# Token groups of 512 and 640 with more staging and scratch buffers, a plain third product and a schedule made anew, in a fused attention and multiplicative feed-forward kernel

## The chip, the cores and the metric

The kernel runs on one core of a Trainium2 chip. The metric is the device time of one execution in microseconds (us), the median of several runs. The profile adds a span, from the first to the last instruction, which is some 1.9 us shorter than the device time. The engines are named as in the profile: PE (TensorE, matmuls), PEld (its weight loads), DVE (VectorE), ACT (ScalarE), POOL (GpSimd), SP (SyncE, which here issues the loads and most of the stores).

## The reference, cut to what matters

```python
q_s = exp(q - max(q));  q_s = q_s / sum(q_s, over head_dim)      # q, k, v: 8 x 8 x 576 x 64
k_s = exp(k - max(k));  k_s = k_s / sum(k_s, over seq)
kv   = einsum('bhsd,bhse->bhde', k_s, v)
attn = einsum('bhsd,bhde->bhse', q_s, kv)
x = attn.transpose(0, 2, 1, 3).reshape(4608, 512)
h = ((x @ w1) * (x @ w2)) @ w3                                   # 512 x 1024, 512 x 1024, 1024 x 1024
out = h @ w_out                                                  # 1024 x 512
```

There are eight batches of 576 tokens, 4608 tokens in all.

## The kernel before

The program first multiplies w3 by w_out once (`W3O`), so that each token needs only `x@w1`, `x@w2`, the product of the two, and one third product with `W3O`. The tokens are worked off in groups. The first group takes its first two products in the plain form. The later groups take them in a form with seven half-width multiplications in place of eight, which costs additional adds on DVE, scratch (`uu`, `cc`) and input combinations (`tt`). In group 4 the third product of eight tiles has such a form as well (`S2S`).

```python
GROUPS = [(0, 576), (576, 576), (1152, 1024), (2176, 640), (2816, 1024), (3840, 768)]
S2S = {4: 4}
HM = max(n for _, n in GROUPS) // 2
tiles("st", 9, [P, 2 * RK * D], F32)      # staging of every load
tiles("tt", 6, [P, 2, HM])
tiles("ab", 18, [P, 1024])
tiles("uu", 5, [P, HM], F32)
tiles("cc", 6, [P, HM])
tiles("ps", 8, [P, 512], F32, psum)

# ... the plain form of the first two products (first group)
for ct in (2 * n, 2 * n + 1):
    nc.tensor.matmul(ps.tile[:, 0:m], lhsT=w[qt][:, ct, fo:fo + P],
                     rhs=x[:, ct, lo:lo + m], start=(ct == 0), stop=(ct == 3))

# ... the third product, plain
for ft in (2 * n, 2 * n + 1):
    nc.tensor.matmul(po.tile[:, :w], lhsT=ab_buf[(g, ft)].tile[:, tb * P:(tb + 1) * P],
                     rhs=W3O[:, ft, m * w:(m + 1) * w], start=(ft == 0), stop=(ft == N_FT - 1))

# ... warm-up matmuls: they compute nothing that is used
def fill(ps, n):
    for _ in range(n):
        nc.tensor.matmul(ps[:, 0:512], lhsT=blank[:, 0:P], rhs=blank, start=True, stop=True)
```

Nothing is scheduled at run time. The tasks (a load, a cast, a pair of matmuls, an eviction) are numbered. A fixed list `ORDER` gives their sequence, `SLOTS` the buffer of each, and `ENGS` the engine of each task that several engines could do.

```python
def run(self, order, slots, engs):
    for b, s in zip(self.bufs, slots):
        b.tile = self.pools[b.pool][s]
    for n in order:
        if isinstance(n, tuple):
            self.fill(self.pools[n[0]][n[1]], n[2])      # warm-up matmuls
        elif self.tasks[n].alts:
            self.tasks[n].emit(engs[n])
        else:
            self.tasks[n].emit()
```

Each engine runs its own instructions in that sequence, so an early instruction that waits holds back all later ones of the same engine.

The softmax here doesn't subtract the row's maximum and nothing guards it: scores larger than these inputs give would overflow.

## Time and profile before

| | before |
|---|---|
| device time, median of the runs beside the changed kernel | 231.76 us (231.07 to 232.23, 4 runs) |
| span of the profiled run, mean granted clock | 230.0 us, 1.0 |
| PE work: useful, warm-up matmuls | 204.0 us, 5.8 us |
| nothing issued on PE | 20.2 us |
| first dense run of first-layer matmuls starts | 33.87 us |

PE work in the table is the order of the PE instructions with columns/2.4 + 3 ns for each, as the prediction derives it. The rest of the span is called unissued: PE had nothing to do, or ran below full pace. Below, the first 34 us are called the head, the handing over from one group of tokens to the next a handover, and what lies between the head and the last third-product matmuls the middle. Here is the memory traffic line of the page of before: GB/s moved in each of 40 equal slices of the span, 5.75 us each.

```profile
GB/s 222 390 404 391 392 388 268 379 330 13 353 371 333 158 242 278 372 50 337 180 211 171 278 278 171 128 111 297 274 204 165 75 0 48 24 68 92 116 131 165
```

After the first slice, the loads run at about 390 GB/s without a break for five slices, to 34.5 us.

### The profile page before, as it was taken

To read this page: it belongs to the slowest core of one execution; us is meant where nothing else is said; L and a number is where in the kernel's file an instruction comes from. 1 tells how busy PE (TensorE), PEld (TensorE's weight loads), DVE (VectorE), ACT (ScalarE), POOL (GpSimd) and SP (SyncE) were. 2 spreads that over 40 slices of the span, in tenths; PEclk is the share of its full clock that TensorE was granted. 3 is DMA by queue.
4 is the path that set the end of the run, shared out by engine and by line. 5 is a ranking of instruction groups with operands and counts; after the bars stand their busy time and mean duration, and the time that the engine had idled before them with its cause. 6 is when DMAs were issued, how large, how long until landed. Compare 5 with 4: busy or idle time off the path is not lost.

```text
span 230.0 us, 5284 instructions
## 1 busy us (share of the span) xinstructions
PE 219.9 (96%) x1971; PEld 124.6 (54%) x1971; DVE 182.8 (79%) x392; ACT 142.0 (62%) x289; POOL 102.2 (44%) x84
## 2 busy tenths in 40 slices
PE   7699999999999999999999999999999899999992
PEld 3354548866676564444445656543444367766640
DVE  0332865789999998999967989999999999889820
ACT  2236875768768998777527658766799474354021
POOL 4313745584064990197940268800299920310000
PEclk9999999999999999999999999999999999999999
DMA  6999997981998679919786976669885502124556
GB/s 222 390 404 391 392 388 268 379 330 13 353 371 333 158 242 278 372 50 337 180 211 171 278 278 171 128 111 297 274 204 165 75 0 48 24 68 92 116 131 165
DMA packets 32888, 50.92 MB, mean 221 GB/s; under 512 B 11744, under 2 KB 12000, under 8 KB 32864
## 3 DMA queue, kind: packets, MB, share of 16 engines
q1 hardware_dynamic: 31504, 48.57, 66.5%
q10 hardware_dynamic: 1360, 2.03, 3.8%
q8 instruction: 15, 0.25, 0.5%
q14 instruction: 9, 0.07, 0.1%
HBM read 38.80 MB, written 9.44 MB: 210 GB/s over the span
## 4 chain that ended last, share of the span: by engine, by line
PE 72%; DVE 10%; DMA 8%; ACT 3%; issue 2%; POOL 2%; SPq 2%; DVEq 0%; ACTq 0%
PE ps L648 31%; PE ps L739 17%; PE ps L591 7%; PE ps L377 6%; PE ps L836 5%; DMA st<-in_moe_w_dram 3%; DMA out_dram<-osb 2%; DMA qsT<-eq 2%; DVE cc L672 2%; PE ps L511 2%; PE ps L556 2%; DVE tt L626 2%; DVE ds L459 1%; POOL eq L469 1%; PE ps L485 1%
## 5 line engine op out<-in xcount | busy, mean ns | idle before, releaser
L672 DVE TENSOR_TENSOR cc<-ps,uu 128x512 f16<-128x512 f32 (+3 forms) x120 | 65.2, 570 | 2.8 <-PE ps L648 0.7
L344 ACT COPY uu<-ps 128x512 f32<-128x512 f32 (+3 forms) x107 | 50.4, 501 | 25.9 <-PE ps L648 14.9
L699 POOL TENSOR_TENSOR ab<-cc,cc 128x512 f16<-128x512 f16 (+3 forms) x25 | 23.1, 927 | 70.2 <-DVE cc L672 59.4
L739 PE MATMUL ps<-W3O,ab 128*128 128x512 f16 (+1 forms) x224 | 53.4, 372 | 0.0
L648 PE MATMUL ps<-tt,wc 128*128 128x512 f16 (+3 forms) x240 | 52.1, 334 | 0.3
L648 PEld LDWEIGHTS <-wc 128*128 128x128 f16 x320 | 31.0, 98 | 25.6 <-DVE tt L626 1.4
L648 PE MATMUL ps<-xt,w 128*128 128x512 f16 (+3 forms) x160 | 36.6, 334 | 0.5 <-ACT osb L725 0.5
L648 PEld LDWEIGHTS <-w 128*128 128x128 f16 x240 | 22.6, 98 | 18.1 <-issue 1.8
L739 PEld LDWEIGHTS <-ab 128*128 128x128 f16 x224 | 21.4, 98 | 20.1 <-issue 0.6
L469 POOL TENSOR_TENSOR eq<-eq,ds 128x1152 f16<-128x1152 f16 x13 | 27.9, 2152 | 6.6 <-DVE ds L466 3.3
L725 ACT ACTIVATE osb<-ps 128x512 f32<-128x512 f32 (+1 forms) x24 | 13.3, 566 | 22.5 <-PE ps L739 19.9
L459 DVE TENSOR_REDUCE ds<-eq 128x9 f32<-128x576 f16 x32 | 23.4, 740 | 4.0 <-ACT eq L455 4.0
L672 DVE TENSOR_TENSOR ab<-ps,cc 128x512 f16<-128x512 f32 (+3 forms) x40 | 22.4, 567 | 1.8 <-PE ps L648 0.6
L455 ACT ACTIVATE eq<-st 128x576 f16<-128x576 f32 x32 | 21.5, 686 | 1.1 <-DMA st<-in_q_dram 1.0
L434 ACT ACTIVATE ek<-st 128x576 f16<-128x576 f32 x32 | 21.0, 688 | 1.6 <-DMA st<-in_k_dram 1.3
L344 ACT CAST xt<-ps 128x320 f16<-128x320 f32 (+7 forms) x46 | 15.4, 400 | 9.1 <-PE ps L556 8.9
L648 PE MATMUL ps<-xt,wc 128*128 128x512 f16 (+3 forms) x80 | 20.2, 334 | 0.0
L648 PE MATMUL ps<-tt,w 128*128 128x512 f16 (+3 forms) x80 | 19.7, 334 | 0.0
L591 PE MATMUL ps<-xt,w 128*128 128x320 f16 (+1 forms) x128 | 16.2, 286 | 0.0
L377 PE MATMUL ps<-ab,ab 128*128 128x512 f16 x64 | 14.8, 379 | 0.4 <-ACT ab L344 0.3
L591 PEld LDWEIGHTS <-w 128*128 128x128 f16 x128 | 12.3, 98 | 3.6 <-issue 0.2
L344 POOL CAST v<-st 128x1152 f16<-128x1152 f32 x10 | 12.5, 1261 | 0.8 <-PE ps L511 0.8
(76 smaller groups left out, 251.6 us busy)
## 6 DMA issues: line engine op xcount, KB each, us to landing
st<-in_q_dram SPq DMA_DIRECT2D x16, 576.0 KB, 5.3
st<-in_v_dram SPq DMA_DIRECT2D x16, 576.0 KB, 8.0
st<-in_k_dram SPq DMA_DIRECT2D x16, 576.0 KB, 7.2
st<-in_moe_w_dram SPq DMA_DIRECT2D x16, 512.0 KB, 8.9
out_dram<-osb SPq DMA_DIRECT2D x56, 128.0 KB, 4.1
st<-in_moe_w_out_dram SPq DMA_DIRECT2D x4, 512.0 KB, 7.5
out_dram<-osb ACTq DMA_DIRECT2D x14, 128.0 KB, 2.4
out_dram<-osb ACTq DMA_DIRECT2D x3, 64.0 KB, 2.5
```

The source lines that it names most:

```text
L344: {"DVE": nc.vector.tensor_copy, "POOL": nc.gpsimd.tensor_copy, "ACT": nc.scalar.copy}[eng](out=o, in_=i)
L377: nc.tensor.matmul(pp.tile, lhsT=wT.tile[:, gt * P:(gt + 1) * P], rhs=wo[i][1].tile[:, (gt % 2) * C:(gt % 2 + 1) * C], start=(gt == 0), st ...
L434: nc.scalar.activation(out=ek.tile[:, :, j, :], func=AF.Exp, in_=vk(bk.tile)[:, j].rearrange("p (r d) -> p r d", r=RK))
L455: nc.scalar.activation(out=eq.tile[:, :, j, :], func=AF.Exp, in_=vq(bq.tile)[:, j].rearrange("p (r d) -> p r d", r=RK))
L459: nc.vector.tensor_reduce(out=ds.tile[:, 0, j], axis=AX.X, op=ALU.add, in_=eq.tile[:, :, j, :])
L469: {"POOL": nc.gpsimd, "DVE": nc.vector}[e].tensor_tensor(out=eq.tile, in0=eq.tile, op=ALU.mult, in1=ds.tile[:, 1].rearrange("p j r -> p r ...
L591: nc.tensor.matmul(ps.tile[:, 0:m], lhsT=w[qt][:, ct, fo:fo + P], rhs=x[:, ct, lo:lo + m], start=(ct == 0), stop=(ct == 3))
L648: nc.tensor.matmul(ps.tile[:, 0:h], lhsT=lhs(c), rhs=rhs(c), start=first and c == 0, stop=c == 1, skip_group_check=not first)
L672: return lambda: nc.vector.tensor_tensor(out=dst(), in0=ps.tile[:, 0:h], in1=other.tile[:, 0:h], op=op)
L699: {"POOL": nc.gpsimd, "DVE": nc.vector}[e].tensor_tensor(out=ab.tile[:, 0:h], in0=c11.tile[:, 0:h], in1=c21.tile[:, 0:h], op=ALU.mult)
L725: nc.scalar.activation(out=o(), in_=i(), func=AF.Copy, scale=ISC)
L739: nc.tensor.matmul(po.tile[:, :w], lhsT=ab_buf[(g, ft)].tile[:, tb * P:(tb + 1) * P], rhs=W3O[:, ft, m * w:(m + 1) * w], start=(ft == 0), ...
```

## The change

The intent: groups of about one batch each, so that less work is bunched at a handover from one group to the next; smaller half widths, whose saved memory pays for more staging and scratch buffers; and a third product in plain form, which spares DVE the combinations.

```diff
-    GROUPS = [(0, 576), (576, 576), (1152, 1024), (2176, 640), (2816, 1024), (3840, 768)]
+    GROUPS = [(0, 512), (512, 640), (1152, 512), (1664, 640), (2304, 512), (2816, 640), (3456, 512), (3968, 640)]
-    S2S = {4: 4}
+    S2S = {}
-    tiles("st", 9, [P, 2 * RK * D], F32)
+    tiles("st", 10, [P, 2 * RK * D], F32)
-    tiles("tt", 6, [P, 2, HM])
+    tiles("tt", 8, [P, 2, HM])
-    tiles("uu", 5, [P, HM], F32)
-    tiles("cc", 6, [P, HM])
+    tiles("uu", 7, [P, HM], F32)
+    tiles("cc", 7, [P, 512])
 # ... cut: helper code for cases that this configuration doesn't use
 # ... cut: ORDER, SLOTS and ENGS are new throughout: another sequence of loads, casts and
 #          matmuls from the first instruction on, and 19 warm-up matmuls in place of 27
```

The last comment matters. The lists were made anew for the new groups, and with them the first 35 us changed, although the loads and casts of the weights, which fill most of that time, do not depend on the groups.

## The prediction

> **What bounds the kernel now.** I read the page's busy line first, then the windows by stage, then the groups by form, then the chain of work that ended last.
>
> The busy line of the page says that PE is the fullest engine and DVE the second:
>
> ```profile
> PE 219.9 (96%) x1971; PEld 124.6 (54%) x1971; DVE 182.8 (79%) x392; ACT 142.0 (62%) x289; POOL 102.2 (44%) x84
> ```
>
> 96% overstates PE, because matmul spans overlap. So I first worked out the pace of PE. Below are one stretch of ten microseconds that holds only 512-column matmuls (columns: stretch and length, then busy and count for PE, PEld, DVE, ACT, POOL, then clock, DMA share, GB/s), and lines of the chain (start, length, what):
>
> ```profile
> 100.00:110.00 10.00, 10.00 (x47) 4.44 (x46) 9.40 (x16) 7.21 (x14) 8.47 (x8) 1.00 0.67 219
> ```
>
> ```profile
> 2.13 7.04 DMA st<-in_moe_w_dram
> ...
> 33.87 14.48 PE ps L591 x118
> ...
> 217.48 8.01 PE ps L739 x42
> 225.53 0.60 ACT osb L725
> ```
>
> 47 matmuls in 10 us is 0.213 us each (0.216 allowing for one at the edge), and 118 of 320 and 256 columns in equal parts take 14.48 us, 0.1227 each. Both fit columns/2.4 ns plus 3 ns. With that pace, the whole instruction order of before is 209.8 us of PE work: weight product 17.5, attention 14.2 (64x64 pieces run four at a time, 72 in 0.78 us), first two products 111.5, third product 60.8, warm-up matmuls 5.8. Laying this work along the timeline leaves 20.2 us with nothing issued: 5.2 in the first 10 us, 2.6 more up to 33.87, 7.8 spread from there to the last matmul (183.7 us of work in the 191.5 us to 225.4), and 4.6 from there to the end. The middle is therefore already tight, and a gain can only come from the unissued time.
>
> Now the stages of before, cut roughly where the groups follow each other:
>
> ```profile
> 34.00:59.00 25.00, 24.81 (x263) 17.28 (x262) 19.43 (x45) 17.11 (x33) 14.11 (x7) 1.00 0.71 251
> 59.00:89.00 30.00, 29.91 (x378) 19.44 (x377) 27.59 (x71) 25.66 (x60) 16.89 (x14) 1.00 0.83 283
> 89.00:125.00 36.00, 35.79 (x313) 16.44 (x310) 31.42 (x56) 23.45 (x43) 18.41 (x12) 1.00 0.74 229
> 125.00:158.50 33.50, 33.04 (x286) 18.41 (x287) 31.23 (x74) 22.71 (x55) 14.84 (x11) 1.00 0.77 203
> 158.50:184.00 25.50, 24.80 (x193) 10.79 (x191) 24.81 (x44) 19.70 (x39) 18.47 (x15) 1.00 0.74 197
> 184.00:217.50 33.50, 33.47 (x243) 23.37 (x240) 30.47 (x72) 14.12 (x37) 4.19 (x5) 1.00 0.24 56
> 0.00:34.00 34.00, 30.15 (x267) 15.05 (x268) 15.10 (x32) 17.19 (x26) 14.34 (x20) 1.00 0.97 364
> ```
>
> The reader should see DVE at 24.81 of 25.5 us in one stage and 31.2 of 33.5 in another, but 19.4 of 25 in the first. DMA is at 0.97 only up to 34 us. So there are three regimes: loads until about 33 us, then PE and DVE together, then a tail of third-product matmuls and stores.
>
> The groups by form give the DVE price against width:
>
> ```profile
> L672 DVE TENSOR_TENSOR cc<-ps,uu 128x512 f16<-128x512 f32 x48 | 31.3, 681 | 0.6 <-ACT uu L344 0.2
> L672 DVE TENSOR_TENSOR cc<-ps,uu 128x384 f16<-128x384 f32 x24 | 12.9, 552 | 1.2 <-PE ps L648 0.5 <-POOL ab L699 0.2
> L672 DVE TENSOR_TENSOR cc<-ps,uu 128x320 f16<-128x320 f32 x24 | 11.0, 483 | 0.2
> L672 DVE TENSOR_TENSOR cc<-ps,uu 128x288 f16<-128x288 f32 x24 | 10.0, 451 | 0.8 <-PE ps L648 0.3 <-ACT uu L344 0.2
> ```
>
> That is 1.03 ns a column plus 155 ns. The durations of all DVE rows sum to 204 us against 182.8 busy, so neighbours overlap by some 54 ns, and an extra instruction really costs about 100 ns.
>
> **What the Trainium skill says.** "TensorE: Matmul & The Clock Gate", section "Back-to-back issue gap", gives an isolated gap of N/2.4 + 2.5 ns and a sustained 131 ns at N=512. The first agrees with this trace, the second does not: 213 to 217 ns here. "VectorE: DVE Perf Modes", the section on the TRN2 errata, says a fixed cost comes with each instruction, (N+151)/0.96 ns for an fp32 add, and advises tiles of 512 or more; the rows above agree (681 ns against its 691). "Perfetto Trace Analysis", section "Optimization Strategy", recommends interleaving regimes with different limits, and says that repeated bubbles can mean too few buffers. Both describe the intent of the change.
>
> **The change, part by part.** Counts are from the built instruction orders of the two kernels.
>
> Third product. The seven-multiplication form in group 4 goes (112 matmuls of 256 columns, 28,672 columns), and 32,768 columns in plain form come in. On PE, third product 60.8 to 62.3 us: +1.5. In return DVE loses 12 combining evictions at 418 ns (5.0 us), 8 half sums (3.3) and 3 scalings (1.3), and POOL loses 12 combinations (17.8 us of its rows).
>
> First two products. The half widths were 288, 512, 320, 512, 384; they become 320 four times and 256 three times. 688 matmuls become 848; PE 111.5 to 111.8 us: +0.3. DVE: 160 evictions of mean width 403 become 224 of mean 293. Their durations rise from 91 to 101 us, about +6 after overlap. Over all rows I get DVE 182.8 to about 191 us, ACT unchanged in sum (161.1 to 161.7 us of durations), and warm-up matmuls from 27 to 19.
>
> Where DVE's extra lies. Splitting the DVE order at the first input combination of group 1: before that point 34.4 us become 40.8; after it 147.8 become 149.3. So most of the extra falls in the load-bound head, where DVE has room.
>
> Head. Before first reaches a dense run at 33.87, with 20.3 us of useful PE work done. After issues two first-layer weight loads ahead of the last attention loads and does 8 matmuls of 512 columns on half of the channels before the second attention piece, so 21.5 us are done when the dense run can start; that start needs the same loaded bytes, so I keep 33 to 33.5 us. Gain about 1.5 us.
>
> Balance of PE and DVE. I summed PE and DVE work from the first matmul of each group to the first of the next:
> - before, groups 1 to 5, PE/DVE: 26.0/26.8, 37.7/30.9, 26.6/30.7, 28.1/27.6, 40.9/31.8. The larger of each pair sums to 164.2 us.
> - after, groups 1 to 7: 27.0/26.3, 20.5/18.9, 26.2/24.8, 15.1/15.6, 30.1/27.8, 14.8/16.0, 29.3/19.9. The larger of each sums to 164.7 us.
>
> PE alone rises from 159.3 to 163.0 there (more of the third product has moved behind group 0), yet the sum of the larger hardly does: the stage in which DVE was 4 us longer than PE is gone. Before took 166 us for it (59.5 to 225.5), 1.8 over the sum. After has seven handovers in place of five, each of one batch and with its attention pieces placed earlier; I allow 2.8.
>
> The sum: dense run from 33.3; group 0 has 21.3 us of PE work left plus 1 for the handover, 55.6; plus 164.7 and 2.8, 223.1; tail 4.3 (last eviction 0.6, then stores, now one whole 512-wide tile), 227.4. The measured time of before lies 2.0 us over its span (231.96 against 230.0), so 229.4 us, some 1% faster.
>
> **The rivals.**
> - *DVE becomes the bound.* With PE/DVE near 1 in six stages, both must be 97% busy together. For it: in 125 to 158.5 us, where DVE led, the stage took 33.5 for 30.7 of DVE work. Against: 158.5 to 184 held both at 24.8 of 25.5 us. If every such stage takes 6% over its larger term, 135.4 us become 143.5 in place of 138.2, and the time is near 235.
> - *The added buffers close nearly all gaps.* ACT waited 8.2 us for DVE before it could fill scratch, and uu goes from 5 to 7, cc 6 to 7, tt 6 to 8, st 9 to 10. If handovers cost nothing and the head gains 2 us more, the time is about 225. Against: PE itself stood still little in these waits.
> - *The waits only move.* Each handover still has exponent, sum, norm (2.15 us on POOL), transpose, product, copy, combination. If each of seven loses the 1.6 us that before's five lost on average (7.8 / 5), the two kernels agree at 231 to 232.
> - *A transfer delays a handover.* The last four batches are transposed by DMA, on a queue shared with loads and stores; one such wait of 4.85 us stood in the chain of before. Two of them would add 2 to 4 us.
>
> **Range and chances.** 229.4 is the sum; the rivals put the edges at 225 and 235, the worse one rarely in full, so 8 times in 10 between 225.3 and 234. Two per cent faster is below 227.4, only 2 us under my sum: 0.30. Slower by over 2% needs over 236.7, beyond DVE as the bound: 0.06. Within 2%: 0.64.
>
> **What would show it.** The dense run should start near 33 us; DVE busy should be 188 to 193 us; there should be no stage from 56 to 195 us in which PE has over 1.5 us unissued, at about 0.4 per handover; pure third product should end near 223 us. If DVE is over 97% busy for long stretches while PE's unissued time exceeds 8 us there, the first rival holds. A dense run that starts at 30 us or at 36 us would make the head term wrong.

## The result, and the profile after

The changed kernel takes 233.97 us (median of 4 runs, 233.79 to 234.41) against 231.76 us. Ratios here are the mean time of one kernel's fast runs over that of the other's of the same rounds, so not quite the ratio of the medians. The ratio is 1.0101, with a 95% interval of 1.0068 to 1.0133: 1% slower, inside the 2% that count as the same. The profiled span is 232.6 us at a clock of 1.0. The prediction was 229.4 us, so its sign was wrong, though its range (225.3 to 234.0) holds the result.

The busy line of the page of the changed kernel, and its memory traffic in 40 slices of 5.8 us:

```profile
PE 219.4 (94%) x2059; PEld 133.4 (57%) x2059; DVE 188.6 (81%) x450; ACT 141.5 (61%) x313; POOL 83.2 (36%) x81
...
GB/s 223 408 319 237 352 391 388 389 391 51 337 393 220 236 137 389 226 247 296 328 195 116 113 190 253 110 310 204 97 290 128 174 133 80 3 45 47 94 91 136
```

DVE stands at 188.6 us, where the prediction had it. The traffic is what differs early on: 319 and 237 GB/s between 11.6 and 23.2 us, where before had 404 and 391.

The chain of work that ended last, in the changed kernel (start, length, what):

```profile
3.13 8.73 DMA st<-in_moe_w_out_dram
11.88 1.98 DVE ab L386 x3
13.87 4.10 DMA st<-in_moe_w_out_dram
18.12 1.28 ACT L386
19.41 1.05 ACT ab L386
23.53 10.72 DMA st<-in_k_dram
37.47 8.36 PE ps L648 x38
...
220.84 6.92 PE ps L817 x32
```

L386 is the cast helper (L344 before), L648 the plain first two products (L591 before), L817 the third product (L739 before). The dense run begins at 37.47 us, not at 33.87. By then 21.5 us of useful PE work are done, against 20.3 in before, so some 2.4 of these 3.6 us are lost time. What leads up to it is a queue of loads, an ACT instruction of 1.28 us, a cast, and the load of the keys. Here are the issues of SP in the changed kernel (start, time from the first to the end of the last of the group, engine, line, operation, target, count):

```profile
3.62 3.36 SPq L333 DMA_DIRECT2D st<-in_moe_w_dram  x3
13.87 0.89 SPq L333 DMA_DIRECT2D st<-in_moe_w_out_dram  x2
16.35 0.37 SPq L333 DMA_DIRECT2D st<-in_q_dram  x1
20.48 0.34 SPq L333 DMA_DIRECT2D st<-in_moe_w_dram  x1
```

Between 6.98 and 13.87 us no load is issued, and again from 16.7 to 20.48. The lists of the two kernels say why. Among the first 13 loads of the changed kernel, staging buffers 1 and 6 are filled three times each, while two of the ten buffers lie unused until the queries and keys come. The load at 20.48 us waits for the first cast of ACT to free buffer 6. That cast waits for its own load, and then for the loading of the activation table, which stands behind the cast's wait in this kernel (18.12 us) and at 0.73 us in before. The page "ScalarE: Activation LUTs" of the Trainium skill, section "What ACT_TABLE_LOAD costs", gives 1283 ns for it; the 1.28 us here agree.

After the head, the stages of the changed kernel look like this (the columns as in the prediction's tables):

```profile
37.50:59.65 22.15, 22.08 (x194) 10.65 (x194) 19.65 (x37) 14.26 (x24) 9.98 (x5) 1.00 0.81 286
59.65:87.00 27.35, 27.35 (x330) 17.31 (x330) 26.16 (x63) 23.12 (x50) 14.49 (x12) 1.00 0.83 269
87.00:108.00 21.00, 20.89 (x172) 15.05 (x171) 18.91 (x51) 17.97 (x42) 5.89 (x8) 1.00 0.83 304
108.00:134.50 26.50, 26.50 (x313) 16.11 (x312) 24.14 (x56) 17.72 (x42) 8.77 (x8) 1.00 0.64 182
134.50:149.50 15.00, 14.91 (x131) 11.25 (x125) 13.81 (x39) 10.80 (x33) 10.20 (x9) 1.00 0.72 200
```

DVE is busy 89 to 96% in these stages, PE in practically all of each, and no stage shows a DVE that is full while PE lags. The groups by form show the price of the narrower evictions:

```profile
L737 DVE TENSOR_TENSOR cc<-ps,uu 128x320 f16<-128x320 f32 x96 | 43.7, 484 | 2.9 <-PE ps L713 2.0 <-ACT uu L386 0.2
L737 DVE TENSOR_TENSOR cc<-ps,uu 128x256 f16<-128x256 f32 x72 | 27.3, 417 | 1.6 <-PE ps L713 0.7 <-ACT uu L386 0.2 <-POOL ab L764 0.2
```

484 ns at 320 columns is what before had (483 ns); there are simply more of them.

**The ledger.** I laid the PE work of every profiled kernel along its own timeline and split the rest of the span at 50 us. "Early" is warm-up matmuls plus unissued time before 50 us, "late" is unissued time after it. A lower clock shows as unissued time here, since the work is priced at full speed; figures are good to some 0.2 us. The rows for the experiments below are added so that all can be compared; each useful-work figure plus early plus late is the span.

| kernel | span | useful PE work | early | late |
|---|---|---|---|---|
| before | 230.0 | 204.0 | 13.4 | 12.6 |
| changed | 232.6 | 205.8 | 15.8 | 11.0 |
| changed, again (c1) | 232.6 | 205.8 | 15.6 | 11.2 |
| e1, e2, e3 | 231.4, 233.2, 231.1 | 205.8 | 14.7, 16.4, 14.3 | 10.9, 11.0, 11.0 |
| e4 | 233.5 | 205.8 | 16.2 | 11.5 |
| e5, e8, e11 | 231.1, 230.3, 230.8 | 205.8 | 14.0, 13.4, 13.8 | 11.3, 11.1, 11.2 |
| e7, e10 | 232.6, 233.4 | 205.8 | 16.0, 16.2 | 10.8, 11.4 |
| e6, e9, e13 | 233.6, 232.8, 231.7 | 205.6 | 13.4, 13.2, 13.2 | 14.6, 14.0, 12.9 |
| e12 | 230.4 | 204.0 | 14.5 | 11.9 |

The row of before agrees with the prediction's own sums, 5.2 + 2.6 us unissued and 5.8 us of warm-ups up to 33.87, then 7.8 + 4.6. The difference of the two spans, 2.6 us, is 2.4 us lost early, 1.8 us of more matmul work, and 1.6 us gained late. So the change did bring a gain behind the head, but less than its added matmul work costs, and it lost 2.4 us in the head. The profiled run of before is a single one, and in e12, whose instructions after 50 us are those of before, late is 11.9 us; so read the gain as some 0.9 to 1.6 us.

The gain lies at the handovers. From the start of the dense run, each group has this unissued time up to the first matmul of the next (the last one up to the last matmul): before 0.8, 1.1, 1.7, 1.6, 2.3 and 0.5 us, 8.0 in all; changed 0.9, 0.4, 0.6, 1.0, 1.3, 0.7, 0.8 and 0.3 us, 6.0 in all. After the last matmul stand 4.5 us in before and 4.9 in the changed kernel.

**Theories.** Mine: the loss lies in the head, in the new sequence of loads and casts, and not in the groups, buffers or forms. The rivals: DVE is the limit of the middle and hides a larger gain; the added buffers matter; the plain third product costs more than its matmul work; and a clock that is granted lower after waits takes a part.

### The profile page after: what moved, and what is told of

Same layout as the page of the kernel before. It is cut to its first block, busy times and chain, and to the rows that moved or that the text cites. A ratio compares the mean times of both kernels' runs of the same rounds, so it can differ in the third digit from the quotient of the medians.

```text
span 232.6 us, 5544 instructions
## 1 busy us (share of the span) xinstructions
PE 219.4 (94%) x2059; PEld 133.4 (57%) x2059; DVE 188.6 (81%) x450; ACT 141.5 (61%) x313; POOL 83.2 (36%) x81
## 4 chain that ended last, share of the span: by engine, by line
PE 79%; DMA 10%; DVE 3%; ACT 2%; SPq 2%; issue 1%; ACTq 0%
PE ps L713 42%; PE ps L817 26%; DMA st<-in_moe_w_out_dram 6%; PE ps L648 5%; DMA st<-in_k_dram 5%; PE ps L563 2%; PE ps L608 2%; SPq L333 2%; PE ps L537 1%; DVE ab L386 1%; DVE tt L690 1%; ACT xt L386 1%; DVE kv L574 1%; DVE osb L792 1%; ACT L386 1%
## 5 line engine op out<-in xcount | busy, mean ns | idle before, releaser
L737 DVE TENSOR_TENSOR cc<-ps,uu 128x320 f16<-128x320 f32 (+1 forms) x168 | 71.0, 456 | 4.6 <-PE ps L713 2.7
L817 PE MATMUL ps<-W3O,ab 128*128 128x512 f16 x288 | 74.6, 379 | 0.0
L386 ACT COPY uu<-ps 128x320 f32<-128x320 f32 (+1 forms) x150 | 54.9, 409 | 31.3 <-PE ps L713 21.0
L713 PE MATMUL ps<-tt,wc 128*128 128x320 f16 (+1 forms) x336 | 57.1, 288 | 0.2
L764 POOL TENSOR_TENSOR ab<-cc,cc 128x320 f16<-128x320 f16 (+1 forms) x32 | 23.4, 738 | 57.0 <-DVE cc L737 57.0
L713 PEld LDWEIGHTS <-w 128*128 128x128 f16 x336 | 32.1, 98 | 14.6 <-issue 0.9
L817 PEld LDWEIGHTS <-ab 128*128 128x128 f16 x288 | 27.5, 98 | 22.1 <-issue 0.5
L713 PE MATMUL ps<-xt,w 128*128 128x320 f16 (+1 forms) x224 | 39.9, 288 | 0.1
L790 ACT ACTIVATE osb<-ps 128x512 f32<-128x512 f32 x26 | 15.1, 598 | 18.9 <-PE ps L817 18.4
L737 DVE TENSOR_TENSOR ab<-ps,cc 128x320 f16<-128x320 f32 (+1 forms) x56 | 24.8, 452 | 0.8
L521 POOL TENSOR_TENSOR eq<-eq,ds 128x1152 f16<-128x1152 f16 x10 | 21.5, 2147 | 10.9 <-DVE ds L518 4.4
L476 ACT ACTIVATE ek<-st 128x576 f16<-128x576 f32 x32 | 21.5, 683 | 4.7 <-DMA st<-in_k_dram 3.7
L713 PE MATMUL ps<-xt,wc 128*128 128x320 f16 (+1 forms) x112 | 22.6, 288 | 0.0
L713 PE MATMUL ps<-tt,w 128*128 128x320 f16 (+1 forms) x112 | 22.3, 288 | 0.0
L386 POOL CAST v<-st 128x1152 f16<-128x1152 f32 x10 | 11.4, 1146 | 21.3 <-DMA st<-in_v_dram 17.0
L386 ACT CAST xt<-ps 128x256 f16<-128x256 f32 (+3 forms) x42 | 14.8, 410 | 6.4 <-PE ps L608 5.8
L648 PE MATMUL ps<-xt,w 128*128 128x512 f16 x64 | 15.1, 379 | 0.6 <-DVE xt L386 0.6
```

Of the source, the lines that this page charges most:

```text
L386: {"DVE": nc.vector.tensor_copy, "POOL": nc.gpsimd.tensor_copy, "ACT": nc.scalar.copy}[eng](out=o, in_=i)
L476: nc.scalar.activation(out=ek.tile[:, :, j, :], func=AF.Exp, in_=vk(bk.tile)[:, j].rearrange("p (r d) -> p r d", r=RK))
L521: {"POOL": nc.gpsimd, "DVE": nc.vector}[e].tensor_tensor(out=eq.tile, in0=eq.tile, op=ALU.mult, in1=ds.tile[:, 1].rearrange("p j r -> p r ...
L713: nc.tensor.matmul(ps.tile[:, 0:h], lhsT=lhs(c), rhs=rhs(c), start=first and c == 0, stop=c == 1, skip_group_check=not first)
L737: return lambda: nc.vector.tensor_tensor(out=dst(), in0=ps.tile[:, 0:h], in1=other.tile[:, 0:h], op=op)
L764: {"POOL": nc.gpsimd, "DVE": nc.vector}[e].tensor_tensor(out=ab.tile[:, 0:h], in0=c11.tile[:, 0:h], in1=c21.tile[:, 0:h], op=ALU.mult)
```

## The experiments

All results are correct unless said otherwise. Each ran beside before on the same chip.

### e1: two staging buffers

Two numbers of `SLOTS`: the load of w3's block 7 goes to buffer 0 in place of 1, the load of w_out's block 2 to buffer 4 in place of 6.

```diff
-  st: w3 block 7 -> 1, w_out block 2 -> 6
+  st: w3 block 7 -> 0, w_out block 2 -> 4
```

> Changed kernel with two staging buffers in the head reassigned (the last weight-3 load goes to the buffer that is unused until the queries, the third output-weight load to the one unused until the keys), so that no buffer is filled three times among the first 13 loads. Head theory: the load queue no longer stands still from 7.0 to 13.9 us; the dense run of first-layer matmuls, at 37.47 us in the changed kernel, starts 2 to 3.5 us earlier, and the time falls from 234.0 to 230.5-232. Rival (the loss lies in the handovers and in DVE after 40 us, the head being refilled anyway): 233.5-234.5, with the dense run earlier or not.

Measured: 233.22 us, ratio to before 1.0110 (1.0056 to 1.0165). The profiled span is 231.4 us, and the dense run starts at 36.21 us. Early time falls from 15.8 to 14.7 us, late time stays, and the traffic of the third and fourth slice rises from 319 and 237 to 398 and 393 GB/s. So in the trace the two buffers are a first part of the head. It is less than the 2 to 3.5 us expected, and the timed runs don't resolve it: the changed kernel itself has 1.0101 and, in c1 below, 1.0114.

### e2: the activation table loaded at the start

```diff
     nc.vector.memset(blank, 0.0)
+    warm = konst.tile([P, 1], F32, name="warm")
+    nc.scalar.activation(out=warm, in_=blank[:, 0:1], func=AF.Exp)
```

> Changed kernel with one 1-column exponential on ScalarE at the start, so that the activation table is loaded at 0.7 us and not at 18.1 us behind the first cast's wait. Head theory: the 1.28 us table load stands in the chain (it ends at 19.4, the cast at 20.5 and the next load issue at 20.5), so 0.8 to 1.3 us earlier dense run and 232.7-233.2 us. Rival: no change, 234.0.

Measured: 234.75 us, ratio 1.0139 (1.0093 to 1.0186), dense run at 37.91 us. Alone it gains nothing: the hole in the loads stays, with 261 and 329 GB/s in the same two slices. In the profiled run the clock was 0.61 and 0.54 in two stretches between 10 and 14 us, which is taken up in e12.

### e3: both

> Both of these edits. Head theory: they partly overlap, because both shorten the wait for the same cast; dense run at 33.5-34.5 us, 230-231.5 us, thus at or a little below before (231.8). Rival: 234.0.

Measured: 233.40 us, ratio 1.0098 (1.0064 to 1.0132), span 231.1 us, dense run at 35.88 us. The memory traffic line of e3:

```profile
GB/s 219 396 402 392 358 395 390 390 207 50 345 395 232 191 183 329 245 298 263 355 208 83 96 264 195 117 340 158 112 302 126 159 135 71 3 45 47 95 91 136
```

The hole at 11.6 to 23 us is gone (402 and 392 GB/s), as in e1, and yet only 1.5 us of the 2.4 came back and the expectation was missed. So the flow of the loads is not all of it; their order was my next guess.

### e4: the whole head of before

The loads, casts, evictions, engines and warm-up matmuls of before's first 40 us, in the changed kernel.

> Changed kernel whose first part (all weight loads and casts, attention of the first batch) is issued in the order, on the engines and with the warm-up matmuls of before, the rest as it is. Head theory: dense run at 33.5-34.5 us as in before (33.87) and everything after it as in the changed kernel: 230-231, below before by 0.3 to 0.8%. Rival: the lost time is in the middle, so 233.5-234.5.

Measured: a wrong result (relative error 0.2), because warm-up matmuls wrote into a PSUM buffer that my new `SLOTS` had given to a live sum. 235.23 us, ratio 1.0168 (1.0125 to 1.0211). The dense run starts at 34.98 us with 46 matmuls in it, but PE stood still from 32 to 34 us for DVE, and after that the clock was 0.50 and 0.66 until 38 us. The test failed as a test of the theory: the sequence of before, put to other groups, has a wait of its own.

### c1: the changed kernel again

> The changed kernel itself, unaltered, as the control on the chip and in the rounds of this call, since the executions of one kernel differ by up to 1% and the first call had no such control. Both theories: ratio to before 1.007 to 1.014.

Measured: 234.30 us, ratio 1.0114 (1.0081 to 1.0147), span 232.6 us. It repeats the result with five rounds, and is the control for e5, e6 and e7.

### e5: the last keys issued ahead of the first weights

e3, and in the sequence of loads:

```diff
-  ... w1 block (0,0), values (0,1), keys (0,1), ...
+  ... values (0,1), keys (0,1), w1 block (0,0), ...
```

> Changed kernel with the two head edits of e3 and, as third, the first first-layer weight load issued after the values and keys of the second half of batch 0 and not before them. Head theory: in e3 the loads never pause, yet the keys land at 32.3 us with 3.5 us of exponent, product, norm and copy behind them; landing earlier by one 0.5 MB load (1.3 us) or more, the dense run starts at 34 to 35 us (37.47 in the changed kernel, 35.88 in e3) and the span falls one for one, to 229-230.3; ratio to the control 0.987 to 0.992. Rival (head hidden): ratio to the control 1.00.

Measured: 233.02 us, ratio 1.0071 (1.0041 to 1.0101), dense run at 35.67 us, early time 14.0 us. That is 0.4% below its control c1 (1.0071 over 1.0114), but the two intervals overlap, and 0.987 to 0.992 was expected. Against e3 the dense run starts only 0.2 us earlier and the span is the same. Behind the keys stand exponent, 36 small matmuls, two norms, a product and a copy, behind a weight one cast; that the order of landing matters is not shown by this run.

### e8: the second half of the first batch's attention pulled forward

e5, and the second cast of values, the two exponents and the 36 matmuls of the second half placed before the weight casts, the copies and most of the first weight matmuls:

```diff
-  POOL: cast w1, cast values(0,1)         ACT: copy qT, copy W3O, copy x, exp keys(0,1)
+  POOL: cast values(0,1), cast w1         ACT: copy qT, copy W3O, exp keys(0,1), copy x
-  PE: x(0,0), 8 x first layer, kv(0,1), x(0,1), dense run
+  PE: x(0,0), kv(0,1), 4 x first layer, x(0,1), dense run
```

> The changed kernel with the edits of e5 and, in the head only, the second half of batch 0's attention pulled forward: its values' cast ahead of the first weight cast on POOL, its two exponents ahead of the first copies out of the combined product on ACT, its 36 products, norms and combined product ahead of most of the first eight 512-column matmuls; every later instruction as it was. Theory (the lost head is the whole of the loss; behind the head the changed kernel is quicker than before): in e5 the PE still had some 1.5 to 2 us of waits between 29 and 35.7 us, all behind these keys; with them gone the span falls from e5's 231.1 to about 229.3, the time to about 231.3, ratio about 1.000, and the useful work done by 45 us matches before's within 1 us. Rival (the time saved in the head is given back at the next handover, because group 1's batch or the weights of the second half aren't there earlier): span stays at 230.6 to 231.2 and the unissued time between 45 and 65 us grows by what the head gained.

The start of the dense run in the timeline of PE (start, length, line, operation, shape, count):

```profile
32.72 1.03 PE L655 MATMUL ps<-xt,w 128*128 128x512 f16 x4
33.67 0.44 PE L615 MATMUL ps<-qsT,kv 64*64 64x64 f16 x8
34.21 9.22 PE L655 MATMUL ps<-xt,w 128*128 128x512 f16 x42
```

Measured: 232.94 us, ratio 1.0071 (1.0053 to 1.0089). The profiled span is 230.3 us, 2.3 less than the changed kernel's and 0.3 over before's; the ledger has early 13.4 us, late 11.1. The early time is that of before (13.4 us), and as expected the useful work done by 45 us is too: 31.4 us, against 31.5. Nothing was given back at the next handover, so the rival of this run falls. The expected median of 231.3 us was missed all the same. The six executions spread over spans of 230.3 to 231.6 at mean clocks of 1.0 down to 0.988, while before's eleven of the same rounds have 228.8 to 229.5 at 0.995 or more, so the profiled run of before at 230.0 us was one of its slower ones. Its median there is 229.2 us, 1.1 us below the best of e8; by device time e8's median is 1.8 us over that of before. What remains is thus not the head by this ledger: 1.8 us of added matmul work stand against 1.5 us gained late. The rest was not traced; the profiled run of before was a slow one, that of e8 a fast one.

### e7: fewer buffers

```diff
-    tiles("st", 10, [P, 2 * RK * D], F32)
+    tiles("st", 9, [P, 2 * RK * D], F32)
-    tiles("tt", 8, [P, 2, HM])
+    tiles("tt", 5, [P, 2, HM])
```

The slots of these two pools were given out anew, each to the buffer that had been free longest, which also takes away the stall of e1.

> Changed kernel with one part undone as far as its order allows: staging buffers 10 back to 9 and combination buffers 8 to 5 (slots given out anew, least recently released first; the scratch buffers can't be fewer in this order, which has 7 alive at once). Theory that these buffers close no gap that counts: ratio to the control 0.99 to 1.003 (the new slots also avoid the triple use in the head, which may win up to 1 us). Rival (they matter for the handovers): 1.005 or more over the control.

Measured: 232.52 us, ratio 1.0071 (1.0024 to 1.0117). Late time is 10.8 us, no more than the changed kernel's 11.0. So the added `st` and `tt` buffers are not where the gain behind the head comes from. (The early 16.0 us of its profiled run hold a stretch at a clock of 0.76 between 30 and 35 us.) The added `uu` and `cc` were not tested alone. The converse, before with all the added buffers, can't be built: it needs 220.8 KB a partition where 207.9 are free. The smaller groups are what makes room.

### e10: less work for DVE

```diff
-                                            in_=eq.tile[:, :, j, :])
+                                            in_=eq.tile[:, :, j, 0:16])
```

Each of 32 sums takes 16 of its 64 terms, so the result is wrong.

> The changed kernel with each of the 32 sums of the query exponents on DVE over 16 of its 64 terms (wrong result on purpose): about 0.45 us less for each, some 14 us less DVE work, nothing else changed. The prediction's balance says that the larger of PE and DVE per group sums to 164.7 us and PE alone to 163.0, so with DVE relieved at most 1.7 us of the balance and a part of the 2.8 us of handovers can go: time falls by 1 to 2.5 us, ratio to before about 1.003 to 1.007. Rival (DVE is the bound behind the head, as the first rival of the prediction has it): time falls by 4 us or more, ratio under 0.995. If it falls by less than 0.5 us, DVE is no limit at all and the unissued 11 us after 50 us are chains of single waits.

```profile
PE 221.7 (95%) x2059; PEld 134.3 (58%) x2059; DVE 176.4 (76%) x450; ACT 141.7 (61%) x313; POOL 83.2 (36%) x81
```

The busy line shows DVE 12.2 us shorter (188.6 to 176.4). Measured: 234.24 us, ratio 1.0149 (1.0126 to 1.0172); late time 11.4 us. Nothing was gained, so DVE is not the bound of the middle, although it is 90% busy there. (This call had no control; the changed kernel's own ratio was 1.0101 and 1.0114 in others.) My own expectation of 1 to 2.5 us fell too. Of the late 11 us, 4.9 stand after the last matmul. For the rest the chain of the changed kernel names single waits for DVE and ACT, near 58, 87, 136 and 152 us, and none of them is one of these sums: that it is such chains, and not a lack of DVE time, fits e10 but was not tested alone.

### e6: only the plain third product, in before

```diff
-    S2S = {4: 4}
+    S2S = {}
```

The eight tiles of group 4 go into the places of the pieces of the other form.

> Kernel before with one part of the change alone: the third product of its group 4 in plain form (64 matmuls of 512 columns in place of 112 of 256, no half sums, no combined evictions), rest as it is. Prediction's sum: +1.7 us of PE work in a stage where PE leads (40.9 against 31.8 us of DVE), so 1.2 to 1.9 us slower, ratio to before 1.005 to 1.008. Rival (DVE and ScalarE relief pays for it): ratio 0.995 to 1.002.

Measured: 235.36 us, ratio 1.0174 (1.0143 to 1.0205): 4.0 us, where the added matmul work is 1.6. DVE falls to 177.2 us and nothing is won by it. The timeline shows where the rest is:

```profile
189.89 2.75 PE L742 MATMUL ps<-W3O,ab 128*128 128x512 f16 x12
...
192.24 0.69 DVE L730 TENSOR_SCALAR osb<-ps 128x512 f32<-128x512 f32 x1 [3.03 <-PE ps L742]
...
193.45 0.48 PE L651 MATMUL ps<-tt,w 128*128 128x384 f16 x2 [0.81 <-DVE tt L629]
```

I had set 12 plain matmuls in a row. DVE sat idle for 3.03 us in front of their eviction, the input combination that PE needed next stood behind it, and PE then waited 0.81 us. So a part of the 4.0 us is my placement.

### e9 and e13: the same, spread

In e9 the 32 pairs of plain matmuls stand one by one between the first-layer matmuls of group 5, with their evictions on ACT and each one pair later.

> Before with the third product of group 4 in plain form as in e6, but the 32 pairs of plain matmuls set one by one at even distances between the first-layer matmuls of group 5 and their eight evictions all on ACT, each one pair later. If e6's 4.0 us were the price of the plain form itself (the loss of small pieces that filled PE's waits), this stays near 1.015 to 1.017. If 1.6 us of them are the added matmul work and the rest was my placement in blocks behind which DVE stood idle, it comes to about 233.1, ratio 1.007, and the unissued time from 185 to 220 us is back near before's 0.1 (+0.6 at most), against 3.1 in e6.

Measured: 234.07 us, ratio 1.0139 (1.0118 to 1.0159), between the two expectations. One wait of PE stands out:

```profile
197.34 1.13 ACTq L718 DMA_DIRECT2D out_dram<-osb  x2
...
198.57 0.86 ACT L347 COPY uu<-ps 128x384 f32<-128x384 f32 x2 [1.26 <-PE ps L651]
199.10 0.49 PE L651 MATMUL ps<-tt,wc 128*128 128x384 f16 x2 [1.34 <-ACT uu L347]
```

ACT spent 1.13 us on issuing two stores, the copies behind them came late, and PE waited 1.34 us. In e13 the ten stores that ACT issued for group 4 go to SP:

```diff
-  ENGS: "ACT"   (ten stores of group 4)
+  ENGS: "SP"
```

> e9 with the ten stores of group 4 that ACT issued moved to the queue of the sync engine. If the plain form costs its added matmul work alone, the wait of 1.34 us at 199 us is gone, the span is 231.0 to 231.7 and the ratio about 1.006 to 1.008. If the plain form costs more (because the half-width pieces filled PE's waits), the wait comes back elsewhere and the ratio stays above 1.011.

Measured: 233.53 us, ratio 1.0098 (1.0081 to 1.0116), span 231.7 us, late time 12.9 us (before: 12.6). The wait is gone. The plain form costs 2.2 us in before (233.53 against 231.34), of which 1.6 are matmul work. The expectation of 1.006 to 1.008 was missed by 0.2 to 0.4%; the remaining 0.6 us I didn't trace to one wait. The three runs together say that some 1.8 us of e6's 4.0 were placement, of the matmuls, the evictions and the stores.

### e12: warm-up matmuls taken out of before

```diff
-  9, 2, 2, 3, 4, 3, 4 warm-up matmuls, in seven places
+  9, 3, 4
```

> Before with the four groups of warm-up matmuls between 5.6 and 12 us taken out (11 of 27). Theory: PE then stands still for 1 to 2 us several times there, the granted clock falls in that stretch in some executions, mean clocks of 0.985 to 0.995 appear, and the median rises by 0.3 to 1 us, ratio 1.001 to 1.005, with a wider spread. Rival: nothing changes, clocks stay at 0.995 or more and the ratio at 1.000, since loads set the pace there and the warm-ups ran in waits.

The windows of before and then of e12 (stretch and length; busy and count of PE, PEld, DVE, ACT, POOL; clock; DMA share; GB/s):

```profile
8.00:12.00 4.00, 2.83 (x25) 1.73 (x26) 2.63 (x5) 2.02 (x2) 1.00 (x1) 1.00 1.04 413
12.00:16.00 4.00, 4.00 (x26) 2.02 (x25) 1.94 (x3) 0.24 (x1) 1.04 (x1) 1.00 1.03 401
```

```profile
8.00:12.00 4.00, 3.17 (x20) 2.07 (x21) 3.19 (x5) 1.93 (x2) 0.02 (x1) 0.50 1.05 416
12.00:16.00 4.00, 4.00 (x20) 2.01 (x19) 1.39 (x2) 1.04 (x1) 1.04 (x1) 0.66 1.04 404
```

With the same instructions but for the warm-ups, and the same loads, the clock is 0.50 and 0.66 where before has 1.00. Eight matmuls of 512 columns take 3.57 us there, and start 0.427 us apart in place of 0.216. These are the waits of PE (in brackets) around the fall of the clock, which the clock record puts at 7.88 us, in e12 and then in before:

```profile
5.56 0.62 PE L369 MATMUL ps<-ident,ab 128*128 128x128 f16 x8 [0.66 <-POOL ab L348]
6.81 0.62 PE L369 MATMUL ps<-ident,ab 128*128 128x128 f16 x8 [0.63 <-POOL ab L348]
8.07 1.91 PE L369 MATMUL ps<-ident,ab 128*128 128x128 f16 x16 [0.65 <-POOL ab L348]
```

```profile
9.06 0.62 PE L365 MATMUL ps<-ident,ab 128*128 128x128 f16 x8 [1.39 <-POOL ab L344]
```

From its first matmul to 14 us PE never waited longer than 0.76 us at once in e12, while before kept its clock through a wait of 1.39 us. What differs is how full PE was: from 4.5 to 7.87 us it was busy 1.64 us in e12 and 2.76 in before. The record has the clock at 0.50 for 6.83 us here; the profiles of c1, e2, e4, e7 and e10 each have one such phase in the head, of 3.41 us. Most of the lost speed is hidden, since the loads set the pace here: the ledger shows 1.1 us more early time. The median of the three fast executions is 232.34 us, against 231.34 for before. Of all six only one has a clock of 0.999 (span 228.9 us), the others 0.980 to 0.984 (230.4 to 233.2 us). Among the fast ones the ratio is 1.0034 (0.9997 to 1.0070), so the time itself stays unclear; the clock does not.

### e11: the waits of e8's head filled with warm-up matmuls

```diff
-  12, 2, 2, 3 warm-up matmuls
+  16, 3, 2, 1, 2, 2, 3
```

> e8 with ten more warm-up matmuls (29 in place of 19), put where its PE waited in the head: four more before the first transpose, three before the first weight product, one and two ahead of waits at 26 and 31 us. They compute nothing. Theory (an idle PE in the head lets the granted clock fall, and that costs the changed family some 0.5 to 1 us in the timed runs): the granted clocks of the executions rise from 0.988 to 1.000 in e8 to 0.995 or more in all, the median falls by 0.4 to 1 us towards 232.1 us, e8's best, ratio near 1.003, while the best execution does not change. Rival (the clock dips come whatever PE does, or warm-ups delay the work behind them): clocks and median stay as in e8, or the best execution gets slower.

Measured: 232.54 us, ratio 1.0054 (1.0035 to 1.0074). All six executions have a clock of 0.995 or more (e8: down to 0.988), and the best is as in e8 (232.03 and 232.12 us). The median lies 1.2 us over that of before, in place of 1.8 in e8, which fits the theory, but the intervals of e8 and e11 overlap. Its interval, unlike e8's, lies below that of c1 (from 1.0081), but not quite below that of the first comparison (from 1.0068): that all edits of the head together win time is likely, and no single one is resolved. It is the best version of the changed kernel, and before is still 0.5% faster. No run points to a version that beats both.

## Why the prediction was wrong, and where it was right

- **Head, the step that failed.** "that start needs the same loaded bytes, so I keep 33 to 33.5 us. Gain about 1.5 us." Measured 37.47 us, 4.2 later, with the 21.5 us of work done as forecast. The bytes are indeed the same: by the start of the dense run 12.3 MB had moved in before, at 364 GB/s on average, and 12.2 MB in the changed kernel, but at 326 GB/s. I counted bytes and not the buffers into which they go, the order in which the engines free them, and what stands behind the one that lands last. All three were in the instruction orders that I had. This term was off by 4.2 us of the 5.2 by which the span (232.6) exceeds the predicted 227.4. The prediction named the test itself: a dense run that starts at 36 us makes the head term wrong. e1, e3, e5 and e8 take 1.1, 1.5, 1.8 and 2.4 us of early time back by small edits of slots, table load and sequence, with the late time unmoved at 10.9 to 11.3. With e8 the early time is that of before (13.4 us), so the loss lay in the new schedule of the head. The gain over before of 1.5 us, which the prediction put here, came in no run.
- **Third product.** The prediction had +1.5 us on PE, +0.3 in the first two products; the work rose by 1.8. In before the plain form costs 2.2 us of time at best (e13), so this term was a little small. The relief for DVE on the other side was worth nothing that these runs show (e6, e10).
- **First two products and DVE.** DVE busy was forecast at 188 to 193 us and is 188.6.
- **Balance of PE and DVE.** From the dense run to the first matmul of group 1 the forecast is 22.3 us, the measurement 22.2. From there to the last matmul the forecast is 164.7 + 2.8 = 167.5, the measurement 168.05 (59.65 to 227.7). The size was right, but e10 speaks against the reason: with 12 us less of DVE work nothing moves. That no stage from 56 to 195 us has over 1.5 us unissued came true (at most 1.3); the 0.4 us for each handover were too few (0.7 on average from group 1 on). The gain of 0.9 to 1.6 us late comes from the regrouping as a whole: the added `st` and `tt` buffers (e7) and the plain form (e13, late 12.9 against 12.6) don't bring it. Whether the shorter groups, their sequence or the added `uu` and `cc` do stays open.
- **Tail.** 4.3 us forecast, 4.9 measured (227.7 to 232.6).
- **Rivals.** DVE as the bound: refuted by e10. The buffers close the gaps: not `st` and `tt` (e7). The waits only move: refuted as to the waits, of which 8.0 us became 6.0 from the dense run to the last matmul. A delayed transfer at a handover: no such wait of microseconds stands in the chain after the head.
- **A reading.** The 5.2 us with nothing issued in the first 10 us are not all idle. The first warm-ups start 0.427 us apart in every kernel, where the price is 0.216. In before there are nine, so some 1.9 us of the 5.2 are matmuls at half pace. (The first clock record of the sixteen traces comes at 3.8 to 7.0 us, so the 1.00 that the pages show before it is no measurement.)
- **Not foreseen.** The clock. Variants of the changed kernel ran at mean clocks down to 0.981, before never below 0.995. In before, thin PE activity in the head brings this about (e12); that it is the same in the changed kernel fits e11, but is not shown. In the first comparison the clocks of the changed kernel were 0.994 to 1.0, so it is no large part of the 1%.

## What to carry to other kernels

When a schedule is made anew, compare the head instruction by instruction, apart from the change that was intended: which buffer each early load takes, what must finish before that buffer is free, and how long a chain hangs on the load that lands last. An engine that is 90% busy is not thereby a bound; take work off it in a run that may be wrong, and see whether the time moves. Warm-up matmuls that compute nothing can keep the granted clock up where the loads leave PE thinly used (e12); that they win time was not resolved here.

## What the Trainium skill lacked or had wrong

- "TensorE: Matmul & The Clock Gate", section "Back-to-back issue gap", gives a sustained 131 ns for 512 columns. Here 38 in a row took 8.36 us and start 216 ns apart; the isolated N/2.4 + 2.5 ns (216 ns) is what a stream shows. The page's section "Wait — 56ns, not 53.3ns?" agrees with this (215.7 ns).
- The same page, section "HAM oscillation — how this bites in real kernels", gives as the rule that PE may have no idle gaps over about 3.4 us. In e12 the granted clock was 0.50 from 7.9 to 14.7 us after three waits of 0.63 to 0.66 us close together, with PE busy 1.64 of the 3.37 us before the fall. So that rule is too lenient for such a stretch; the page's next section does report a fall with frequent short idles, but gives no length and no busy share.
- No page says that a table load can hang behind the wait of the first ACT instruction. Here it began at 18.12 us in place of 0.73, though loading it early gained nothing alone (e2).
